# Where the zero stores stand: a mixture-of-experts layer behind chunked attention, with the gating of the last row tiles and the first loads put in another order

## The chip, the cores and the metric

The kernel runs on one core of a Trainium2 chip. The metric is the time of one execution on the device in microseconds (us); the kernel before takes 282.58 us (median of three runs, 282.15 to 282.78). A core has TensorE (PE, with its weight loads as PEld), VectorE (DVE), ScalarE (ACT), GpSimd (POOL) and SyncE (SP), which here only issues DMAs. Each engine works through its own list of instructions in order, and semaphores tie the lists together.

## The reference

`q`, `k`, `v` are 8 x 8 heads of 576 positions by 64 numbers. Attention is taken within chunks of 64 positions; its output, 4608 tokens of 512 numbers, goes through a mixture of 8 experts. A token belongs to the expert with the largest logit, an expert takes at most `capacity` (80) tokens, those with the largest gate, and all other rows of the output are zero.

```python
scores = scale * np.matmul(q_c, k_c.transpose(0, 1, 2, 4, 3))   # chunks of 64
attn = softmax(scores)
x = (attn @ v_c) as rows of 512                                 # 4608 tokens
...
logits = x @ w_gate
expert_idx = np.argmax(logits, axis=1)
gate_w = softmax(logits)[np.arange(N), expert_idx]
out = np.zeros((N, D), dtype=np.float32)
for e in range(E):
    tok_idx = the at most `capacity` tokens of expert e with the largest gate
    h = np.maximum(x[tok_idx] @ w1[e], 0.0)                     # 512 x 1024
    out[tok_idx] = gate_w[tok_idx, None] * (h @ w2[e])          # 1024 x 512
```

## The kernel before, in words

The work has three stages, one behind the other on the PE.

**Attention and gating (to about 140 us).** The tokens are 36 row tiles of 128, `i` = 0 to 35, and four of them make a group T. A load `n` brings two row tiles (`load`, L308): the queries (L318) and, for each of the two head parities, keys and values (L321), into one of four buffers `tok`. The parity's rows go to every other partition, so the other halves must be zero: `blank` (L764) clears them once at the start. The loop at L812 runs one row tile after another through a pipeline: scores of tile i (`start_scores`, L338, into `s`), attention times values of i-2 (`start_values`, L357, into `o`, copied to `x` by `keep`, L389), transposing the scores of i-1 and exp (`probs`, L382 and L384), transposing the result of i-3 (`xtrans`, L416, copied to `xT` at L417), and on DVE the maximum and the difference for tile i (`weights_of`, L368 and L371). Every fourth tile takes the logits of a group (`gate_mm`, L428; `gate_copy`, L440), normalizes it (`sums`, L396 and L398), which also stores it to the DRAM scratch `xs` from POOL (L403, L408), and transposes the logits back (`gate_sum`, L449). What follows on DVE for a group are eleven small operations: `lh` (L456), `lg` (L459) and the nine of `gate` (L506), of which the second hands an exp to ACT (L480). They are not written into the loop but wait in a list `gates`; another list, `bounds_q`, holds the search for the capacity threshold and the counting of levels (`levels` L528 to L533, `signs` L538 on ACT, `steps_` L543, `tally` L553 and L556 on PE, `left_add` L681). `fill` (L298) takes three entries from the two lists; `weights_of` calls it five times and `sums` twice, so that these small steps go between the large ones. `EARLY` (L45) says behind which tile the first six 1 MB pieces of expert weights are loaded (L759).

The loop is followed by an order written out by hand (L840 to L898): the last two tiles go through the pipeline, `gate_sum(28, 4)` puts the operations of tiles 28 to 31 aside (`late`), the token buffers are freed (L856) and SP loads w2 of expert 1 and both weights of expert 2 (`part`, L860, issued at L871). Then the small operations of tiles 28 and 32 are taken in turns, by the letters of `LAST` (L40), and all level steps follow.

**Choosing (to about 164 us).** From the threshold (`ge`, L697) over masks and ranks to the row numbers of the tokens that are kept. `keep_warm` (L727) puts matmuls without use on PE between them. All is manually ordered; an engine's instructions come in the order of the text.

**Experts (to the end).** The 8 experts have 96 slots each, six groups `r` of 128 rows, so a group takes up to three experts. `experts` (L171) gathers all six groups from `xs` by indirect DMA from POOL (L177), scales and transposes them (L188, L200), and runs layer 1 in two halves (L211, `hc`) and layer 2 (L244, `yc`), scales by the gate (L249, `ysc`) and scatters to `out` (L250). SP's loads are issued in the hook `ahead` (L1011): weights of experts 3 to 7 in the order of need, each into a buffer that the tokens or an earlier expert left, the first behind the first gather (a one-column copy by DVE, L870, carries that dependence). Between them stand the nine stores `out<-zero` (`clear`, L735, issued at L738) that put zeros into the whole output; the scatters wait for all nine.

The lists around the change, as the kernel has them:

```python
EARLY = {7: [0], 13: [1], 19: [2], 25: [3], 30: [4], 33: [5]}
...
for e, l in (((3, 0), (3, 1), (4, 0), (4, 1)), ((5, 0),), ((5, 1), (6, 0)),
             ((6, 1), (7, 0)), ((7, 1),), (), (), ())[r]:
    part(e, l, xg[0][:, 0:1] if (e, l) == (3, 0) else None)
if r < 2:
    for n in ((0, 1, 2, 3), (4, 5, 6, 7, 8))[r]:
        clear(n)
```

`(e, l)` is layer l + 1 of expert e; `ahead(0)` runs behind the gathers, `ahead(r + 1)` behind the matmuls of round r.

Of the kernel before, what the change touches and what calls it, by code (L numbers as in the profile page):

```python
# [12 lines left out]
ALU = mybir.AluOpType  # L13
# [25 lines left out]
LV, LP = 7, 8  # L39
LAST = "aaabababababababababab"  # L40
LEVEL_BY = "vavavavv"
HALVES = 32
HOT = 8

EARLY = {7: [0], 13: [1], 19: [2], 25: [3], 30: [4], 33: [5]}  # L45

# [16 lines left out]
def attention_moe(ctx: ExitStack, tc: tile.TileContext, q, kv, wg, w1, w2, cap, cst, out):  # L63
# [107 lines left out]
    def experts(pool, pp, gi, si, gate, getw, tag, extra=None):  # L171
# [64 lines left out]
        def layer2(r):  # L236
            y = (pp.tile([P, DM], F32, name=f"y{tag}{r}", tag="h", bufs=4) if extra and r == NR - 1
                 else pp.tile([P, DM], F32, name=f"y{tag}{r}", tag="y", bufs=1))
            for c in range(8):
                if c == 4 and extra and r == NR - 2:  # L240
                    hpose(NR - 1)
                for g in range(4):
                    o = 32 * g
                    nc.tensor.matmul(  # L244
                        y[o:o + 32, :], lhsT=hT[r][c // 4][:, c % 4, o:o + 32],
                        rhs=getw(groups[r][g])[1][:, c, :],
                        start=(c == 0), stop=(c == 7), tile_position=(0, o))
            ys = pool.tile([P, DM], F32, name=f"ys{tag}{r}", tag="ys", bufs=3 if extra else 1)
            nc.vector.tensor_scalar(ys, y, gate[:, r:r + 1], None, op0=ALU.mult)  # L249
            nc.gpsimd.indirect_dma_start(  # L250
                out=out, out_offset=bass.IndirectOffsetOnAxis(ap=si[:, r:r + 1], axis=0),
                in_=ys, in_offset=None, bounds_check=NT * 512 - 1, oob_is_err=False)
# [26 lines left out]
    with ExitStack() as actx:  # L279
# [28 lines left out]
        def load(n):  # L308
# [8 lines left out]
            def move(r0, r1, engs):  # L317
                engs[0].dma_start(t[:, r0:r1, 0:512], q[T, :, 2 * b + r0:2 * b + r1])  # L318
                for h in range(2):
                    c = 512 + KV * h  # L320
                    engs[1 + h].dma_start(t[h:P:2, r0:r1, c:c + KV],  # L321
                                          kv[T, h, :, 2 * b + r0:2 * b + r1])
            if n == 0:
                move(0, 1, (nc.sync, nc.sync, nc.scalar))
                move(1, 2, (nc.scalar, nc.sync, nc.sync))
            elif n == 1:
                move(0, 1, (nc.sync,) * 3)
# [34 lines left out]

        def weights_of(i):

# [398 lines left out]
        with tc.manual_schedule():  # L763
            def blank(n, r0, r1, eng):  # L764
                eng.memset(tok[n][:, r0:r1, 512:QKV], 0.0)
            blank(0, 0, 1, nc.vector)
            blank(0, 1, 2, nc.gpsimd)
            load(0)
            nc.scalar.dma_start(ident, cst[:, C_ID:C_ID + P])
            warm = gk.tile([P, 2 * P], BF16, name="warm", tag="lv", bufs=LV)  # L770
            nc.vector.memset(warm, 0.0)
            blank(1, 0, 1, nc.vector)
            blank(1, 1, 2, nc.gpsimd)
            blank(2, 0, 2, nc.vector)
            blank(3, 0, 2, nc.gpsimd)
            pw = ps2.tile([P, 256], F32, name="pw", tag="g")
# [35 lines left out]
            for i in range(RT):  # L812
# [10 lines left out]
                if i >= 3:  # L823
                    xtrans(i - 3)
                weights_of(i)
                if i >= 7 and i % 4 == 3:
# [11 lines left out]
                for n in EARLY.get(i, ()):  # L838
                    early_weights(n)
            vc = nc.vector.tensor_copy  # L840
            start_values(34)
            keep(34)
            probs(35)
            xtrans(33)
            flush(gates)
            gate_sum(28, 4)
            late = list(gates)
            gates.clear()
            sums(8, 0, 2)
            start_values(35)  # L850
            keep(35)
            flush(bounds_q)
            xtrans(34, "pt")
            xtrans(35, "m", vc)
            sums(8, 2, 4)
# [4 lines left out]
            def part(e, l, after=None):  # L860
# [10 lines left out]
                nc.sync.dma_start(w[l], (w1, w2)[l][e].rearrange("(c p) f -> p c f", p=P))  # L871
            for e, l in ((1, 1), (2, 0), (2, 1)):
                part(e, l)
            gate_mm(32, 4)
            gate_copy(32, 4)
            tails = {"a": deque(late), "b": gates}
            gate_sum(32, 4)
            for w, rt in (("a", 28), ("b", 32)):
                levels(tails[w], rt, 4)
            keep_warm(24)  # L880

            def count(rt, way):
                for j in range(rt, rt + 4):
                    if LEVEL_BY[j - 28] == way:
                        if way == "a":
                            signs(j)
                        else:
                            steps_(nc.vector, j)
            tails["a"].append((count, (28, "a")))
            tails["b"].append((count, (32, "a")))  # L890
            for w in LAST:
                step_one(tails[w])
            for w in "ab":
                flush(tails[w])
            for rt in (28, 32):
                count(rt, "v")
            for fn in S.pop('late'):
                fn()  # L898
            io_h = wk.tile([P, P, HOT], BF16, name="io_h", tag="x", bufs=3)
            nc.scalar.copy(io_h, io_b[:, P:2 * P, None].to_broadcast([P, P, HOT]))  # L900
            left_add(28, 4)
            tally(32, 4)
# [100 lines left out]
    with tc.manual_schedule():  # L1003
        with ExitStack() as ectx:
# [6 lines left out]
            def ahead(r, xg):  # L1011

                for e, l in (((3, 0), (3, 1), (4, 0), (4, 1)), ((5, 0),), ((5, 1), (6, 0)),
                             ((6, 1), (7, 0)), ((7, 1),), (), (), ())[r]:
                    part(e, l, xg[0][:, 0:1] if (e, l) == (3, 0) else None)
                if r < 2:
                    for n in ((0, 1, 2, 3), (4, 5, 6, 7, 8))[r]:
                        clear(n)

            experts(ep, pp, lambda r: gi1[:, r - 1:r] if r else gi0, si, gate, weights.get, "c",  # L1020
# [158 lines left out]
```

## Time and profile before

| | before |
|---|---|
| median of 3 runs | 282.58 us (282.15 to 282.78) |
| the profiled execution | 283.28 us |
| its span, first to last instruction | 281.5 us |
| mean granted TensorE clock | 0.951 |
| busy: PE, PEld, DVE, ACT, POOL | 249.1, 155.4, 117.6, 94.5, 57.5 us |
| DMA moved | 84.88 MB, 302 GB/s on average |
| weight loads of 2 MB | 13, 19.0 us from issue to landing (median) |

All times below are from the profiled execution, counted from its first instruction. The page gives busy time by engine, 40 equal slices of the span, the DMA queues, the chain of work that ended last, the costliest groups of instructions (`line engine operation out<-in xcount`) and the DMA issues. A row of a timeline reads: start, duration, engine, line, operation, out<-in, shape, count of merged instructions, and in brackets the engine's idle time before it and what ended it. "SPq" and "POOLq" are issues of DMAs. A DMA's "us to landing" counts from its issue until its data is there.

### The profile page before, as it was taken

How to read it: one execution, taken by the hardware profiler on the slowest of the kernel's cores; microseconds unless marked ns; L12 is line 12 of the kernel's file. 1: busy time of each engine (PE TensorE's matmuls, PEld its weight loads, DVE VectorE, ACT ScalarE, POOL GpSimd, SP SyncE). 2: the span in 40 equal slices, each digit the busy share in tenths (PEclk: the TensorE clock that was granted, in tenths of full speed). 3: DMA queues.
4: the chain of work that ended last, by engine and by line, in shares of the span. 5: the costliest groups of instructions: out<-in, count | busy, mean ns of one | idle time of the engine just before them, and what ended most of it. 6: DMA issues, size and time to landing. Idle time of an engine off the chain costs nothing. (4 is left out here: it accounts for less than half of the span.)

```text
span 281.5 us, 6470 instructions
## 1 busy us (share of the span) xinstructions
PE 249.1 (88%) x2703; PEld 155.4 (55%) x2703; DVE 117.6 (42%) x345; ACT 94.5 (34%) x194; POOL 57.5 (20%) x115
## 2 busy tenths in 40 slices
PE   4499999999999998799969969999969929999980
PEld 2488787978797877598746833333313303323320
DVE  6553465656476767437288550202010010111210
ACT  1036555556557667547825011202002001101000
POOL 9201103020202026811345360000000111010011
PEclk9999999999999999979995979999988986999997
DMA  4999899999999999640899369999999999910000
GB/s 137 350 378 398 286 352 381 381 363 406 334 386 403 349 401 367 269 154 1 239 413 408 143 200 387 398 393 404 416 403 406 404 402 400 394 72 10 3 35 34
DMA packets 31987, 84.88 MB, mean 302 GB/s; under 512 B 2576, under 2 KB 2704, under 8 KB 31952
## 3 DMA queue, kind: packets, MB, share of 16 engines
q1 hardware_dynamic: 28128, 71.32, 67.7%
q0 software_dynamic: 3456, 12.49, 11.6%
q10 hardware_dynamic: 368, 0.59, 0.9%
q8 instruction: 23, 0.38, 0.5%
q14 instruction: 12, 0.10, 0.1%
HBM read 64.07 MB, written 20.59 MB: 301 GB/s over the span
## 5 line engine op out<-in xcount | busy, mean ns | idle before, releaser
L211 PE MATMUL hc<-w,xtc 128*32 128x512 f32 x384 | 50.1, 647 | 8.2 <-SPq L1024 6.0
L338 PE MATMUL s<-tok 128*64 128x128 f32 x576 | 40.9, 287 | 4.2 <-DMA tok<-in_kv 4.2
L244 PE MATMUL yc<-w,htc 128*32 128x512 f32 x384 | 42.3, 592 | 0.0
L368 DVE TENSOR_REDUCE mx<-s 128x8 f32<-128x512 f32 x36 | 24.8, 688 | 36.8 <-PE s L338 36.3
L338 PEld LDWEIGHTS s<-tok 128*64 128x64 f32 x576 | 32.3, 141 | 13.8 <-issue 13.7
L357 PE MATMUL o<-tok,pT 128*64 128x130 f32 x576 | 38.7, 276 | 0.0
L211 PEld LDWEIGHTS hc<-w,xtc 128*32 128x32 f32 x384 | 12.7, 117 | 39.8 <-issue 29.5
L389 ACT COPY x<-o 128x520 f32<-128x520 f32 x36 | 21.3, 591 | 37.7 <-PE o L357 37.7
L357 PEld LDWEIGHTS o<-tok,pT 128*64 128x64 f32 x576 | 33.3, 137 | 1.1 <-ACT xT_last L417 0.8
L216 ACT ACTIVATE hsc<-hc 128x512 f32<-128x512 f32 x6 | 3.6, 598 | 77.9 <-PE hc L211 77.9
L244 PEld LDWEIGHTS yc<-w,htc 128*32 128x32 f32 x384 | 12.4, 110 | 28.3 <-issue 28.3
L250 POOL DMA_INDIRECT out<-ysc,si x6 | 6.0, 994 | 100.1 <-DMA out<-zero 53.3
L371 DVE TENSOR_TENSOR sm<-s,mx 128x512 f32<-128x512 f32 x36 | 24.8, 688 | 0.5
L382 PE MATMUL pt<-ct,sm 128*128 128x128 f32 x144 | 24.0, 290 | 0.0
L384 ACT ACTIVATE pT<-pt 128x512 f32<-128x512 f32 x36 | 21.5, 598 | 6.5 <-PE pt L382 5.5
L416 PE MATMUL px<-ct,x 128*128 128x128 f32 x144 | 21.9, 277 | 0.0
L417 ACT COPY xT<-px 128x512 f32<-128x512 f32 x32 | 18.6, 581 | 6.3 <-PE L L428 6.1
L382 PEld LDWEIGHTS pt<-ct,sm 128*128 128x128 f32 x144 | 15.4, 143 | 6.3 <-issue 6.1
L249 DVE TENSOR_SCALAR ysc<-yc,gatec 128x512 f32<-128x512 f32 x6 | 4.5, 751 | 33.5 <-PE yc L244 33.5
L233 DVE COPY htc<-hpc 128x512 f32<-128x512 f32 x6 | 4.2, 692 | 33.4 <-PE hpc L229 33.4
L416 PEld LDWEIGHTS px<-ct,x 128*128 128x128 f32 x144 | 17.2, 144 | 0.0
L218 DVE TENSOR_SCALAR hsc<-hc 128x512 f32<-128x512 f32 x6 | 4.1, 692 | 25.0 <-PE hc L211 25.0
(164 smaller groups left out, 255.5 us busy)
## 6 DMA issues: line engine op xcount, KB each, us to landing
w<-in_w SPq DMA_DIRECT2D x13, 2048.0 KB, 19.0
tok<-in_kv SPq DMA_DIRECT2D x32, 516.0 KB, 6.7
out<-zero SPq DMA_DIRECT2D x9, 1024.0 KB, 16.0
xs<-x POOLq DMA_DIRECT2D x8, 1040.0 KB, 10.3
tok<-in_q SPq DMA_DIRECT2D x16, 512.0 KB, 8.6
w<-in_w SPq DMA_DIRECT2D x6, 1024.0 KB, 9.4
tok<-in_kv SPq DMA_DIRECT2D x7, 258.0 KB, 5.8
xs<-x POOLq DMA_DIRECT2D x4, 260.0 KB, 9.1
```

The source lines that it names most:

```text
L211: nc.tensor.matmul(h[o:o + 32, :], lhsT=xT[r][:, b, o:o + 32], rhs=getw(groups[r][g])[0][:, b, 512 * f:512 * f + 512], start=(b == 0), sto ...
L244: nc.tensor.matmul(y[o:o + 32, :], lhsT=hT[r][c // 4][:, c % 4, o:o + 32], rhs=getw(groups[r][g])[1][:, c, :], start=(c == 0), stop=(c == ...
L250: nc.gpsimd.indirect_dma_start(out=out, out_offset=bass.IndirectOffsetOnAxis(ap=si[:, r:r + 1], axis=0), in_=ys, in_offset=None, bounds_ch ...
L338: nc.tensor.matmul(U[i]['s'][64 * u:64 * u + 64, pr], lhsT=qt[:, pr, u, :], rhs=kt[:, :, c:c + 64], start=True, stop=True)
L357: nc.tensor.matmul(po[64 * u:64 * u + 64, pr // 2, o:o + 130].rearrange("p (h e) -> p h e", h=2), lhsT=U[i]['pT'][:, pr, 64 * u:64 * u + 6 ...
L368: nc.vector.tensor_reduce(mx, d['s'], axis=AX.X, op=ALU.max)
L371: nc.vector.tensor_tensor(sm.rearrange("p c k h -> p c h k"), d['s'], mx[..., None].to_broadcast([P, 4, 2, 64]), op=ALU.subtract)
L382: nc.tensor.transpose(pt[:, pr, :], sv[:, pr, :], ident)
L384: nc.scalar.activation(pT, pt, AF.Exp, scale=0.125)
L389: copy(TT[T]['x'][:, r].rearrange("p (a c) e -> p a (c e)", a=2), U[i]['po'][:, :, 0:260])
L416: nc.tensor.transpose(pm[:, pr, :], t['x'][:, r, pr, 1:129], ident)
L417: copy(t['xT'][:, :, P * r:P * r + P], pm)
```

## The change

It has four parts.

1. The nine zero stores leave the experts' stage. A new table `CLEAR` puts them behind the token tiles 29 to 35, the first right behind the last token load, in turns with the last two early weight pieces. w1 of expert 3 is loaded with the weights of experts 1 and 2, ahead of the gather; w2 of expert 3 is now the first load behind the gather.
2. The first token load is issued by SP alone, in the order row 0, row 1; only the identity matrix is still loaded by ACT. The blanks of the first buffers are split between DVE and POOL by head parity, that of the third buffer goes to POOL whole and that of the fourth to ACT, as a copy of a zero column.
3. The loop ends ahead of `weights_of(35)`. The rest is written out anew: no small steps between the last row tile's operations; tiles 28 to 31 go through their gating and levels ahead of the last transposes (ACT copies both of these, DVE that of tile 33), their counting ahead of `gate_sum(32, 4)`; then come the operations of tiles 32 to 35 alone, with 12 instead of 24 `keep_warm` matmuls.
4. The last group's scaling by the gate is split between ACT and DVE.

```diff
-LAST = "aaabababababababababab"
...
-EARLY = {7: [0], 13: [1], 19: [2], 25: [3], 30: [4], 33: [5]}
+EARLY = {7: [0], 13: [1], 19: [2], 25: [3], 30: [4], 31: [5]}
+CLEAR = {29: [0], 30: [1], 31: [2], 32: [3, 4], 33: [5, 6], 34: [7], 35: [8]}
...
-            nc.vector.tensor_scalar(ys, y, gate[:, r:r + 1], None, op0=ALU.mult)
+            g = gate[:, r:r + 1]
+            if extra and r == NR - 1:
+                nc.scalar.activation(ys[:, 256:DM], y[:, 256:DM], AF.Copy, scale=g)
+                nc.vector.tensor_scalar(ys[:, 0:256], y[:, 0:256], g, None, op0=ALU.mult)
+            else:
+                nc.vector.tensor_scalar(ys, y, g, None, op0=ALU.mult)
...
-            if n == 0:
-                move(0, 1, (nc.sync, nc.sync, nc.scalar))
-                move(1, 2, (nc.scalar, nc.sync, nc.sync))
-            elif n == 1:
+            if n < 2:
                 move(0, 1, (nc.sync,) * 3)
                 move(1, 2, (nc.sync,) * 3)
...
-        def weights_of(i):
+        def weights_of(i, fill=fill):
...
-            def blank(n, r0, r1, eng):
-                eng.memset(tok[n][:, r0:r1, 512:QKV], 0.0)
-            blank(0, 0, 1, nc.vector)
-            blank(0, 1, 2, nc.gpsimd)
+            def blank(n, r0, r1, eng, h0=0, h1=2):
+                eng.memset(tok[n][:, r0:r1, 512 + KV * h0:512 + KV * h1], 0.0)
+            blank(0, 0, 1, nc.vector, 0, 1)
+            blank(0, 0, 1, nc.gpsimd, 1, 2)
+            blank(0, 1, 2, nc.vector, 0, 1)
+            blank(0, 1, 2, nc.gpsimd, 1, 2)
             load(0)
...
-            blank(1, 0, 1, nc.vector)
-            blank(1, 1, 2, nc.gpsimd)
-            blank(2, 0, 2, nc.vector)
-            blank(3, 0, 2, nc.gpsimd)
+            blank(1, 0, 2, nc.vector, 0, 1)
+            blank(1, 0, 2, nc.gpsimd, 1, 2)
+            blank(2, 0, 2, nc.gpsimd)
+            nc.scalar.copy(tok[3][:, :, 512:QKV],
+                           warm[:, 0:1].to_broadcast([P, 2, 2 * KV]))
...
+                if i == 35:
+                    break
                 weights_of(i)
...
+                for n in CLEAR.get(i, ()):
+                    clear(n)
             vc = nc.vector.tensor_copy
+            for n in CLEAR[35]:
+                clear(n)
+            weights_of(35, lambda: None)
+            gate_mm(28, 4)
+            gate_copy(28, 4)
+            probs(35)
             start_values(34)
             keep(34)
-            probs(35)
-            xtrans(33)
+            xtrans(33, copy=vc)
             flush(gates)
+            sums(7)
             gate_sum(28, 4)
-            late = list(gates)
-            gates.clear()
-            sums(8, 0, 2)
             start_values(35)
             keep(35)
-            flush(bounds_q)
+            sums(8, 0, 2)
+            levels(gates, 28, 4)
+            flush(gates)
             xtrans(34, "pt")
-            xtrans(35, "m", vc)
+            xtrans(35, "m")
             sums(8, 2, 4)
             qx.close()
...
-            for e, l in ((1, 1), (2, 0), (2, 1)):
+            for e, l in ((1, 1), (2, 0), (2, 1), (3, 0)):
                 part(e, l)
             gate_mm(32, 4)
             gate_copy(32, 4)
-            tails = {"a": deque(late), "b": gates}
-            gate_sum(32, 4)
-            for w, rt in (("a", 28), ("b", 32)):
-                levels(tails[w], rt, 4)
-            keep_warm(24)
...
-            tails["a"].append((count, (28, "a")))
-            tails["b"].append((count, (32, "a")))
-            for w in LAST:
-                step_one(tails[w])
-            for w in "ab":
-                flush(tails[w])
-            for rt in (28, 32):
-                count(rt, "v")
+            flush(bounds_q)
+            for way in "av":
+                count(28, way)
+            left_add(28, 4)
+            gate_sum(32, 4)
+            levels(gates, 32, 4)
+            keep_warm(12)
+            flush(gates)
+            for way in "av":
+                count(32, way)
...
-            left_add(28, 4)
             tally(32, 4)
...
-                for e, l in (((3, 0), (3, 1), (4, 0), (4, 1)), ((5, 0),), ((5, 1), (6, 0)),
+                for e, l in (((3, 1), (4, 0), (4, 1)), ((5, 0),), ((5, 1), (6, 0)),
                              ((6, 1), (7, 0)), ((7, 1),), (), (), ())[r]:
-                    part(e, l, xg[0][:, 0:1] if (e, l) == (3, 0) else None)
-                if r < 2:
-                    for n in ((0, 1, 2, 3), (4, 5, 6, 7, 8))[r]:
-                        clear(n)
+                    part(e, l, xg[0][:, 0:1] if (e, l) == (3, 1) else None)
```

## Prediction

> **What bounds the kernel now.** I read the page first, then the chain of waits, then the timeline of PE in the experts' stage, then the DMA issues of SP and the DMA traffic by window.
>
> ```profile
> span 281.5 us, 6470 instructions
> ...
> out<-zero SPq DMA_DIRECT2D x9, 1024.0 KB, 16.0
> ```
>
> The chain that ended last runs over PE matmuls of the experts (L211, L244) from 232.88 us to the last scaling, and before that hangs on a load. So the end is set by TensorE, and the question is only where TensorE is kept waiting. In its own timeline:
>
> ```profile
> 205.67 1.03 PE L211 MATMUL hc<-w,xtc 128*32 128x512 f32 x6
> 208.85 5.32 PE L211 MATMUL hc<-w,xtc 128*32 128x512 f32 x26 [2.14 <-DMA w<-in_w]
> ...
> 215.56 3.64 PE L211 MATMUL hc<-w,xtc 128*32 128x512 f32 x32
> ...
> 225.88 1.03 PE L211 MATMUL hc<-w,xtc 128*32 128x512 f32 x4
> 232.88 5.53 PE L211 MATMUL hc<-w,xtc 128*32 128x512 f32 x28 [5.97 <-SPq L1024]
> ```
>
> The undisturbed half of layer 1 (32 matmuls) takes 3.64 us. The first half for row group 3 runs from 205.67 to 208.85 + 5.32 = 214.17, that is 8.50 us: 4.86 us lost, part waiting and part at half speed after the wait. For row group 4 it runs from 225.88 to 232.88 + 5.53 = 238.41, 12.53 us: 8.89 us lost. Together 13.75 us. The first names a weight load as releaser; the second names a sequencer at the program's last `If`, which can't release a matmul here, so I take it for the weight load of expert 6 too. Why are the weights late? SP issued this:
>
> ```profile
> 108.02 1.10 SPq L759 DMA_DIRECT2D w<-in_w  x2
> 133.27 41.50 SPq L871 DMA_DIRECT2D w<-in_w  x7
> 174.87 17.31 SPq L738 DMA_DIRECT2D out<-zero  x4
> 192.29 2.66 SPq L871 DMA_DIRECT2D w<-in_w  x1
> 194.99 14.31 SPq L738 DMA_DIRECT2D out<-zero  x5
> 209.40 22.52 SPq L871 DMA_DIRECT2D w<-in_w  x5
> ```
>
> Four zero stores stand ahead of w1 of expert 5 (the load of 192.29) and five more ahead of what follows; each is 1 MB, 2.6 us at the 400 GB/s of that stage. The buffers were not what it waited for: w1 of expert 5 goes where expert 0's lay, whose last reader was done near 175 (166.37 + 4.67, a row below, and another 3.64). Between 108 and 133 SP has nothing to issue, and the traffic (40 slices of 1.525 us from 104 to 165) shows what DMA does then; below it, the us from issue to landing of weights, small stores of x and gathers of token rows:
>
> ```profile
> GB/s 401 408 376 361 338 371 419 414 255 3 0 262 385 52 11 0 0 0 5 16 208 306 314 234 373 422 420 417 419 425 411 402 396 389 340 52 0 5 185 55
> ...
> w<-in_w SPq DMA_DIRECT2D x3, 2048.0 KB, 14.6
> ...
> xs<-x POOLq DMA_DIRECT2D x4, 260.0 KB, 9.1
> ...
> xgc<-xs,gic POOLq DMA_INDIRECT x3, 3.6
> ```
>
> DMA is nearly empty from 117.7 to 134.5 and again from 157 to 165.
>
> **Part 1: zero stores and one weight load moved.** Nine stores leave the experts' stage (9.44 MB) and stand behind the last token load (about 108); w1 of expert 3 (2.10 MB) moves ahead of the gather. Nothing queues behind a new wait on SP: the zero tile is set at the start, and the two early weight loads mixed among the stores are first read after 166. The weights of experts 1 and 2 follow in the same queue.
>
> In the experts' stage nine loads remain, 5.2 us each at 400 GB/s. Even if the first starts only at 170 (below), w1 of expert 5 lands near 191, of 6 near 206 (w2 of 5, ahead of it, must wait until layer 2 of group 0 frees its buffer), of 7 near 221, against needs at about 208, 224 and 239 (205.67; 225.88 less the first wait of 4.86; their distance less that wait, 15.35, further on; each 2.6 later by the other parts). The smallest margin is some 17 us, so both waits go whole: **−13.75**, bounds −13.75 and −11 (if a shorter wait turned up elsewhere). Nothing else is late next: the rest is matmuls back to back.
>
> The cover for the moved bytes is not complete. From 104 to 165 the DMA moved about 15.0 MB (the GB/s row times 61 us); 11.5 MB more make 26.5 MB, and at 400 GB/s these end near 170, where before the weights were in by 158. The first gather is issued in the middle of that:
>
> ```profile
> 160.11 1.17 POOL L177 DMA_INDIRECT xgc<-xs,gic  x1 [3.94 <-DVE bt L951]
> ```
>
> ```profile
> 164.67 0.15 DVE L870 COPY w<-xgc 128x1 f32<-128x1 f32 x1
> ```
>
> ```profile
> 166.37 4.67 PE L211 MATMUL hc<-w,xtc 128*32 128x512 f32 x32
> ```
>
> Before, it landed 3.6 us after its issue, at 163.7; DVE, with other work until then, came to it at 164.67. Under load, from 165 on, the same page part for 165 to 260 reads:
>
> ```profile
> xgc<-xs,gic POOLq DMA_INDIRECT x4, 7.5
> out<-ysc,si POOLq DMA_INDIRECT x4, 6.3
> ```
>
> With 7.5 us (the same operation, the same load) the rows are there at 167.6 instead of 164.67: **+2.9**. Bounds: +1.7 by the scatter's 6.3, and +4.5 by the 9.1 us of the small stores of x. The stores of x themselves meet the same load, but the last is issued near 144 and has until 160.
>
> [...]
>
> **Part 2: first loads.**
>
> ```profile
> 1.23 1.78 DVE L765 MEMSET tok<- 128x2064 f32 x1 [1.23 <-PEq L1168]
> ```
>
> ```profile
> 3.03 2.11 SPq L321 DMA_DIRECT2D tok<-in_kv  x3
> ```
>
> ```profile
> 3.04 0.56 ACTq L321 DMA_DIRECT2D tok<-in_kv  x1
> 3.63 0.60 ACTq L318 DMA_DIRECT2D tok<-in_q  x1
> ```
>
> ```profile
> 10.56 1.76 PE L338 MATMUL s<-tok 128*64 128x128 f32 x14 [4.19 <-DMA tok<-in_kv]
> ```
>
> ```profile
> tok<-in_kv ACTq DMA_DIRECT2D x1, 258.0 KB, 3.4
> ```
>
> The first scores start at 10.56, released by a key/value load. Those of row 0 were issued at 3.03 and 3.04, and one of them took 3.4 us, so the start waits for the last of row 1 as well (issued until 5.14). Split between DVE and POOL the first blank takes half of 1.78, so the first key/value load goes out 0.89 us sooner, at 2.1; four more issues at about 0.62 put the last one's start at 4.6. Landing ends: 8.0 (3.4 us later, alone) and 9.67 (all as before, only 0.89 sooner). I take 8.6, nearer the first, because the constants and the second queue no longer mix with these bytes: **−2.0**, bounds −0.9 and −2.6. PE is the limit from there to the last row tile, since the token loads are eight row tiles ahead, so the gain stays. The fourth buffer's blank moves to ACT, which has nothing to compute until 16.
>
> **Part 3: the last row tiles.** Before, DVE did the gating chains of tiles 28 and 32 together, in turns:
>
> ```profile
> 141.28 0.37 ACT L440 COPY lt<-L 128x256 f32<-128x256 f32 x1 [0.45 <-PE L L428]
> 144.30 0.23 ACT L480 ACTIVATE ex<-sh 128x32 f32<-128x32 f32 x1 [2.65 <-DVE sh L479]
> ```
>
> ```profile
> 142.22 0.42 DVE L442 COPY lt<-L 128x256 f32<-128x256 f32 x1 [0.47 <-PE L L428]
> 142.56 0.41 DVE L456 TENSOR_TENSOR lh<-lT,x 128x256 f32<-128x256 f32 x1
> 143.00 0.62 DVE L459 TENSOR_REDUCE lg<-lh 128x32 f32<-128x256 f32 x1
> ```
>
> ```profile
> 142.69 0.44 PE L449 MATMUL lT<-ct,lt 128*128 128x128 f32 x2 [0.17 <-DVE lt L442]
> ```
>
> ```profile
> 146.84 0.18 DVE L488 TENSOR_TENSOR keys<-comp,gg 128x32 f32<-128x32 bf16 x1
> 147.05 0.19 DVE L528 TENSOR_TENSOR bv<-keys,lob 128x32 f32<-128x32 f32 x1
> 147.28 0.24 DVE L531 TENSOR_TENSOR bv<-bv,inw 128x32 f32<-128x32 f32 x1
> 147.55 0.18 DVE L533 TENSOR_REDUCE bo<-bv 128x4 f32<-128x32 f32 x1
> 147.65 1.06 DVE L543 TENSOR_SCALAR lv<-io_b,bo 128x256 bf16<-128x256 bf16 x5
> ...
> 149.13 0.17 DVE L697 SCALAR_TENSOR_TENSOR ge<-ph,left 128x16 bf16<-128x16 f32 x1 [0.33 <-PE ph L556]
> ```
>
> From the transposed logits of tile 32 (lT, 142.69) to the threshold (ge, 149.13) it took 6.4 us. Alone the chain is 0.41 + 0.62 + twelve steps at 0.21 (the spacing of the first two rows of the last fence), 3.55 us; then three level steps instead of five (0.6), tally and threshold (0.7): from 0.44 after lT begins, 5.3 us, a gain of 1.1. But lT comes later. In the new order, by the clock of before: DVE copies the transpose of tile 33 (0.69) until 138.0; eight short steps and a reciprocal of the queues that were left, then lh, lg and two normalizing steps of 28 bring it to 141.2; two steps more give ACT its exp, and ACT's copies of the transposes of 34 and 35 stand behind that exp, so they end at 142.8 (before: 141.4). DVE ends the chain of 28 at 143.7, normalizes (0.45) and copies lt until 144.6; two sums, two level steps and the tally of 28 stand ahead of lT on PE, which begins at 145.5 instead of 142.69. That is 2.8 later, less 1.1 gained: **+1.65**, bounds −1.1 (lT not later) and +2.6 (PE, with half the warming matmuls, at the half speed that the 232.88 row shows after a wait). The steps within are all of DVE and ACT, so no DMA load changes them.
>
> **Part 4: last scaling.**
>
> ```profile
> 273.30 0.75 DVE L249 TENSOR_SCALAR ysc<-yc,gatec 128x512 f32<-128x512 f32 x1 [6.12 <-PE yc L244]
> ```
>
> Half of it on DVE (0.42 for 256 columns, the lt row) beside half on ACT (0.37): **−0.33**, between 0 and −0.4; the scatter waits for both.
>
> **Sum.** −13.75 + 2.9 − 2.0 + 1.65 − 0.33 = −11.5. The profiled execution took 283.28 (1.78 around its span) and would take 271.8, a span of 270.0; it was 0.70 above the median of the three runs, 282.58, for which the sum gives **271.0**.
>
> **Rivals.**
> - *The gather isn't slowed.* [...] For it: stores of x under load (9.1) overtook weights issued about then (14.6). Against it: 7.5. Time 271.0 − 2.9 = 268.1.
> - *The first loads don't gain.* One queue issues the two loads that ACT issued beside it (0.56 + 0.60 = 1.16 us), more than the 0.89 gained: +0.3 instead of −2.0, 273.3. For it: SP's issues are back to back from 3.03. Against: landing, not issuing, took most of the 10.56. [...]
> - *The gather waits for all that was issued ahead of it*, until 170, landing near 171 and not 167.6: 274.4. Against: the same 9.1 beside 14.6.
> - *Slower: loads of SP starve the gathers of POOL.* The second gather (needed near 176) would come only in a gap of SP's queue, the first being where w2 of expert 5 waits for its buffer; that is after nine us of PE work and five loads, near 193: 17 us late, 288. It decides once a gather under load takes over 19 us (7.5 + 11.5). Against: 7.5 with SP's queue full.
> - *The change doesn't do what it says*: the zero stores were not what kept the weights. Then the waits stay and the other terms add up: 271.0 + 13.75 = 284.8. Against: the order of issue above.
>
> **How the numbers follow.** Chances: forecast 0.57, gather not slowed 0.14, first loads don't gain 0.14, gather behind everything 0.10, starved 0.03, waits stay 0.02. The forecast's own bounds together (gather −1.2/+1.6, head −0.6/+1.1, last tiles −2.75/+0.95) rarely all fall one way; 266.5 to 275.0 holds it and the next three cases, and leaves out the last two and the sums of extremes. 0.2% is 0.57 us, about what a measurement of this kernel tells from no change. Faster 0.94, same 0.01, slower 0.05.
>
> **What would show it.** PE in the experts' stage has no idle time over 1 us from the first layer 1 to the last; the nine stores are issued from about 106 and traffic stays near 400 GB/s until 168; the first gather takes 6 to 8 us; the first scores start between 8 and 9.7; from the first scores to ge takes longer by 1 to 2 us. Wrong would be: a wait of L211 or L244 for w, a token load that lands later than its scores, or a gather at 4 us.

## The result and the profile after

The changed kernel takes 273.01 us (median of four executions, 271.69 to 274.25) beside 282.68 (282.15 to 284.90) for the kernel before, a ratio of 0.964 (0.958 to 0.971): 9.7 us faster. The prediction said 271.0 (266.5 to 275.0). The profiled execution took 272.99; its span is 271.2, 10.3 less than before.

First the page of the changed kernel. The last column of the group rows is the idle time of PE just before such instructions.

```profile
span 271.2 us, 6450 instructions
...
L211 PE MATMUL hc<-w,xtc 128*32 128x512 f32 x384 | 45.0, 612 | 0.0
...
L244 PE MATMUL yc<-w,htc 128*32 128x512 f32 x384 | 42.3, 592 | 0.0
```

PE never waits for a weight: both layers have no idle time before them. PE's timeline shows the two places that had lost 4.86 and 8.89 us:

```profile
168.90 5.27 PE L211 MATMUL hc<-w,xtc 128*32 128x512 f32 x32
...
208.81 3.62 PE L211 MATMUL hc<-w,xtc 128*32 128x512 f32 x32
...
224.14 3.62 PE L211 MATMUL hc<-w,xtc 128*32 128x512 f32 x32
```

The first half of layer 1 now takes 3.62 us in groups 3 and 4, the undisturbed time. SP's queue (start, time until the last of the run is issued):

```profile
108.20 0.60 SPq L740 DMA_DIRECT2D out<-zero  x1
...
112.45 22.50 SPq L740 DMA_DIRECT2D out<-zero  x7
135.05 89.65 SPq L885 DMA_DIRECT2D w<-in_w  x13
```

The zero stores are issued by 135 and thirteen weight loads follow with no store between them. The DMA traffic from 104 to 165, in the same 40 slices as for the kernel before, has no gap left; below it, from the same window, the count, size and median us from issue to landing:

```profile
GB/s 394 401 380 327 246 357 403 420 416 391 419 422 400 413 419 400 389 404 408 407 406 418 388 407 403 312 363 398 376 353 343 396 371 410 422 415 399 389 384 396
...
w<-in_w SPq DMA_DIRECT2D x4, 2048.0 KB, 25.4
...
xs<-x POOLq DMA_DIRECT2D x4, 260.0 KB, 12.4
...
xgc<-xs,gic POOLq DMA_INDIRECT x4, 7.5
```

The gather is issued into that traffic, and DVE, which copies a column of its rows, waits for it:

```profile
159.33 1.17 POOL L177 DMA_INDIRECT xgc<-xs,gic  x1 [3.93 <-DVE bt L961]
```

```profile
167.21 0.15 DVE L884 COPY w<-xgc 128x1 f32<-128x1 f32 x1 [3.38 <-DMA xgc<-xs,gic]
```

The marks at the head, at the last row tile and at the end, from PE's, DVE's, ACT's and POOL's timelines:

```profile
10.51 0.91 PE L340 MATMUL s<-tok 128*64 128x128 f32 x6 [4.13 <-DMA tok<-in_kv]
...
129.77 1.09 PE L340 MATMUL s<-tok 128*64 128x128 f32 x16
...
254.66 7.91 PE L244 MATMUL yc<-w,htc 128*32 128x512 f32 x72
```

```profile
148.32 0.17 DVE L699 SCALAR_TENSOR_TENSOR ge<-ph,left 128x16 bf16<-128x16 f32 x1 [0.40 <-PE ph L558]
...
263.15 0.48 DVE L252 TENSOR_SCALAR ysc<-yc,gatec 128x256 f32<-128x256 f32 x1 [6.62 <-ACT ysc L251]
```

```profile
262.64 0.47 ACT L251 ACTIVATE ysc<-yc,gatec 128x256 f32<-128x256 f32 x1 [10.32 <-PE yc L244]
```

```profile
263.91 0.98 POOL L255 DMA_INDIRECT out<-ysc,si  x1 [6.12 <-DVE ysc L252]
```

Of the kernel before, two marks are still missing, from PE's and POOL's timelines (its last layer-2 matmul ended at 273.24, 0.06 ahead of its scaling):

```profile
131.25 1.09 PE L338 MATMUL s<-tok 128*64 128x128 f32 x16
```

```profile
274.33 0.98 POOL L250 DMA_INDIRECT out<-ysc,si  x1 [5.88 <-DVE ysc L249]
```

Cut at these marks, the two spans compare like this:

| stretch, us | before | after | difference | predicted |
|---|---|---|---|---|
| start to first scores | 10.56 | 10.51 | -0.05 | -2.0 |
| to the scores of tile 35 | 120.69 | 119.26 | -1.43 | 0 |
| to `ge` | 17.88 | 18.55 | +0.67 | +1.65 |
| to the first gather's issue | 10.98 | 11.01 | +0.03 | 0 |
| to DVE's first use of its rows | 4.56 | 7.88 | +3.32 | +2.9 |
| to the first layer 1 | 1.70 | 1.69 | -0.01 | 0 |
| to the end of the last layer 2 | 106.87 | 93.67 | -13.20 | -13.75 |
| to the last scatter's issue | 1.09 | 1.34 | +0.25 | -0.33 |
| to the end of the span | 7.17 | 7.29 | +0.12 | 0 |

The large terms are as predicted. The first loads, the last scaling and an unforeseen -1.43 in the token stage are not.

### The profile page after: what moved, and what is told of

It reads as the page before. It is cut to its first block, busy times and chain, and to the rows that moved or that the text cites. A ratio compares the mean times of both kernels' runs of the same rounds, so it can differ in the third digit from the quotient of the medians.

```text
span 271.2 us, 6450 instructions
## 1 busy us (share of the span) xinstructions
PE 241.2 (89%) x2691; PEld 151.6 (56%) x2691; DVE 115.0 (42%) x345; ACT 98.3 (36%) x196; POOL 57.8 (21%) x116
## 4 chain that ended last, share of the span: by engine, by line
PE 80%; DMA 10%; ACT 3%; DVE 2%; POOL 2%; issue 1%; POOLq 0%; ACTq 0%
PE hc L211 16%; PE yc L244 15%; PE s L340 13%; PE o L359 11%; PE pt L384 7%; PE px L418 5%; DMA xs<-x 4%; PE L L430 3%; DMA xgc<-xs,gic 3%; PE hpc L229 2%; DMA tok<-in_kv 2%; ACT lv L540 2%; POOL tok L767 1%; PE xpc L200 1%; PE lT L451 1%; PE pwarm L734 1%
## 5 line engine op out<-in xcount | busy, mean ns | idle before, releaser
L211 PE MATMUL hc<-w,xtc 128*32 128x512 f32 x384 | 45.0, 612 | 0.0
L211 PEld LDWEIGHTS hc<-w,xtc 128*32 128x32 f32 x384 | 12.0, 112 | 27.4 <-issue 27.0
L254 DVE TENSOR_SCALAR ysc<-yc,gatec 128x512 f32<-128x512 f32 x5 | 3.8, 752 | 27.3 <-PE yc L244 27.3
L499 POOL TENSOR_TENSOR comp<-comp,ct 128x32 bf16<-128x32 bf16 x18 | 3.9, 233 | 48.1 <-DVE comp L513 41.2
## 6 DMA issues: line engine op xcount, KB each, us to landing
w<-in_w SPq DMA_DIRECT2D x6, 1024.0 KB, 10.3
```

Source lines behind the costliest of these rows:

```text
L211: nc.tensor.matmul(h[o:o + 32, :], lhsT=xT[r][:, b, o:o + 32], rhs=getw(groups[r][g])[0][:, b, 512 * f:512 * f + 512], start=(b == 0), sto ...
```

## The experiments

Each kernel is the changed one with the edit shown, if nothing else is said; times are medians of six executions (twelve of the last head experiment), with the ratio to the kernel before run beside them.

### Part 1 alone, on the kernel before

```diff
-EARLY = {7: [0], 13: [1], 19: [2], 25: [3], 30: [4], 33: [5]}
+EARLY = {7: [0], 13: [1], 19: [2], 25: [3], 30: [4], 31: [5]}
+CLEAR = {29: [0], 30: [1], 31: [2], 32: [3, 4], 33: [5, 6], 34: [7], 35: [8]}
...
+                for n in CLEAR.get(i, ()):
+                    clear(n)
...
-            for e, l in ((1, 1), (2, 0), (2, 1)):
+            for e, l in ((1, 1), (2, 0), (2, 1), (3, 0)):
...
-                for e, l in (((3, 0), (3, 1), (4, 0), (4, 1)), ((5, 0),), ((5, 1), (6, 0)),
+                for e, l in (((3, 1), (4, 0), (4, 1)), ((5, 0),), ((5, 1), (6, 0)),
...
-                if r < 2:
-                    for n in ((0, 1, 2, 3), (4, 5, 6, 7, 8))[r]:
-                        clear(n)
```

> The kernel before with part 1 of the change alone (zero stores behind tiles 29 to 35, (3,0) ahead of the gather, (3,1) first behind it). Theory: all of the gain is part 1's. By the two traces the experts' stage gives 13.2 and the gather takes back 3.3, so 9.9 faster than the kernel before: 273.1 (272.5 to 273.8), with no wait of PE for weights from the first layer 1 to the end. Rival (the other parts carry some of it): 274.5 or more.

273.26 us, 0.965 (0.962 to 0.969), against the whole change's 0.964 (0.958 to 0.971). All that PE waits for between 165 and 262, in the view of waits (total, times, longest), is the gather's rows:

```profile
PE xpc L201 <- DVE xnc L189: 5.2, 1, 5.2
```

So part 1 carries the gain, and the other three parts together move the time by nothing that can be told.

### The loads that stand in the gather's way

```diff
-            for e, l in ((1, 1), (2, 0), (2, 1), (3, 0)):
+            for e, l in ((1, 1),):
...
-                for e, l in (((3, 1), (4, 0), (4, 1)), ((5, 0),), ((5, 1), (6, 0)),
+                for e, l in (((2, 0), (2, 1), (3, 0), (3, 1), (4, 0), (4, 1)), ((5, 0),), ((5, 1), (6, 0)),
```

> The change, but with the loads of (2,0), (2,1) and (3,0) taken from ahead of the gather to behind it, (2,0) now the one that waits for it; (1,1) stays early. Theory (the first gather shares the DMA engines with the weights): the last early load, (1,1), lands at about 158, so the engines are empty when the gather is issued at about 159.3; it lands after 3.6 to 4.5 us instead of 7.9, layer 1 starts about 3.4 us earlier, the weights come 4 to 5 us later than in the changed kernel, which its 5 to 16 us of slack takes in, and the time falls from 273.0 to 269.6 (269 to 270.3). Rival A (the gather is late for another reason, such as its rows' stores to xs): it still takes 7 to 8 us and the time is 273.0 or above. Rival B (the loads are only just in time): the gather is quick, but waits of layer 1 and layer 2 for weights come back, over 1 us each, and the time is 271.5 to 274.

273.29 us, 0.967 (0.964 to 0.969): no gain. The gather, issued at 159.30, was used at 163.96 (DVE's timeline), 3.2 us less than in the changed kernel, which settles that it paid for the traffic beside it:

```profile
163.96 0.15 DVE L884 COPY w<-xgc 128x1 f32<-128x1 f32 x1 [0.17 <-issue]
```

Where the gain went stands in PE's timeline:

```profile
165.40 5.34 PE L211 MATMUL hc<-w,xtc 128*32 128x512 f32 x32
...
205.98 1.03 PE L211 MATMUL hc<-w,xtc 128*32 128x512 f32 x6
208.75 3.62 PE L211 MATMUL hc<-w,xtc 128*32 128x512 f32 x26 [1.73 <-DMA w<-in_w]
```

Layer 1 started 3.5 us earlier (165.40 instead of 168.90). At group 3 PE waited for w1 of expert 5, and group 4 began where it had in the changed kernel (224.08, 224.14). With the engines kept empty for the gather's sake (122 GB/s from 162 to 166), the later loads moved back: DMA, at 384 to 399 GB/s from 172 to 230, is the bound behind PE. Rival B of the expectation was right on this. The next kernel holds back two loads instead of three:

```diff
-            for e, l in ((1, 1), (2, 0), (2, 1), (3, 0)):
+            for e, l in ((1, 1), (2, 0)):
...
-                for e, l in (((3, 1), (4, 0), (4, 1)), ((5, 0),), ((5, 1), (6, 0)),
+                for e, l in (((2, 1), (3, 0), (3, 1), (4, 0), (4, 1)), ((5, 0),), ((5, 1), (6, 0)),
```

> The change, but with (2,1) and (3,0) alone taken behind the gather; (2,0) stays early. Theory (DMA is the bound until about 230, so an idle stretch of it moves all later weights by its length, and the gather is slow only while weights are in flight): (2,0) lands at about 164, the gather between 4 and 5.5 us after its issue, the engines idle some 3 us instead of the 8 in the experiment that holds three, (5,0) lands at about 204, ahead of its need at about 206: 1.5 to 2.5 us faster than the change, 270.5 to 271.5. Rival A (a single 2 MB load in flight slows the gather as much): 6.5 to 8 us for the gather, 272.5 to 273. Rival B (the weights again come too late): a wait of over 1 us in layer 1 of group 3, 272 to 273.

270.65 us, 0.958 (0.955 to 0.961): 2.4 us faster than the change. The gather, issued at 160.44, was used 4.58 us later, and group 3 ran without a wait:

```profile
166.46 3.64 PE L211 MATMUL hc<-w,xtc 128*32 128x512 f32 x32
...
204.74 3.80 PE L211 MATMUL hc<-w,xtc 128*32 128x512 f32 x32
```

One 2 MB load less to make up for (5.2 us at 400 GB/s) decides between no gain and most of it. Whether a single load in flight would slow the gather was not tried: here the last one was nearly done when the gather was issued.

### The last row tiles in the order of before

```diff
-                if i == 35:
-                    break
...
+            probs(35)
...
+            late = list(gates)
...
+            for w in LAST:
+                step_one(tails[w])
```

> The change, but with the last row tiles in the order of before (part 3 undone; the ninth zero store stays behind tile 35). Theory from the two traces (scores of tile 35 to ge 17.88 us before, 18.55 us after): 0.7 us faster, 272.3. The prediction's size: 1.65 faster, 271.4. Rival (part 3 is a gain, or nothing, and the difference lay in single executions): 273.0 or slower, with 18.3 us or more from the scores of tile 35 to ge.

273.54 us, 0.965 (0.963 to 0.968): by the time alone, the same as the change. The stretch itself says more. From PE's and DVE's timelines, 131.49 to 149.38:

```profile
131.49 1.09 PE L341 MATMUL s<-tok 128*64 128x128 f32 x16
```

```profile
149.38 0.17 DVE L700 SCALAR_TENSOR_TENSOR ge<-ph,left 128x16 bf16<-128x16 f32 x1 [0.33 <-PE ph L559]
```

This is 17.89 us. The three profiled kernels with the order of before have 17.87 to 17.89, the six with the changed order, leaving out those that move the sums (below), 18.38 to 18.63. So part 3 costs 0.5 to 0.75 us. The time of this execution (273.56) doesn't show it, because it lost 1.3 us ahead of this stretch, where the granted clock was 0.60 from 120 to 124 (below).

### The last scaling on DVE alone

```diff
-            if extra and r == NR - 1:
-                nc.scalar.activation(ys[:, 256:DM], y[:, 256:DM], AF.Copy, scale=g)
-                nc.vector.tensor_scalar(ys[:, 0:256], y[:, 0:256], g, None, op0=ALU.mult)
-            else:
-                nc.vector.tensor_scalar(ys, y, g, None, op0=ALU.mult)
+            nc.vector.tensor_scalar(ys, y, g, None, op0=ALU.mult)
```

> The change, but with the last group's scaling by the gate on DVE alone (part 4 undone). Theory (the halves run one behind the other, DVE waits for ACT): the end of the last matmul to the last scatter's issue takes 1.1 us instead of 1.34, and the time is 0.25 faster, 272.75. Rival (the prediction's term): 0.33 slower, 273.3.

272.37 us, 0.963 (0.960 to 0.965): 0.6 us below the change, less than the spread of either kernel's times (2.6). PE ended at 261.37; then, in DVE's timeline and POOL's:

```profile
261.44 0.75 DVE L250 TENSOR_SCALAR ysc<-yc,gatec 128x512 f32<-128x512 f32 x1 [6.12 <-PE yc L244]
```

```profile
262.47 0.98 POOL L251 DMA_INDIRECT out<-ysc,si  x1 [5.88 <-DVE ysc L250]
```

1.10 us from the end of PE to the scatter, against 1.34 with the split. The rows of the change show why: ACT's half ran from 262.64 to 263.11, and DVE's began at 263.15, named as released by ACT. Two halves one behind the other (0.47 + 0.48) are longer than the whole (0.75). That is an order of the program: DVE's half waits for the semaphore that ACT's half raises, so the chip was never asked to do both at once. Both halves read one PSUM tile, and no run here shows what they would do there without the wait. Whether halves in two tiles would overlap was not tried.

### The first loads

```diff
-            if n < 2:
+            if n == 0:
+                move(0, 1, (nc.sync, nc.sync, nc.scalar))
+                move(1, 2, (nc.scalar, nc.sync, nc.sync))
+            elif n == 1:
...
-            blank(0, 0, 1, nc.vector, 0, 1)
-            blank(0, 0, 1, nc.gpsimd, 1, 2)
+            blank(0, 0, 1, nc.vector)
+            blank(0, 1, 2, nc.gpsimd)
```

> The change, but with the first loads and the blanks of before (part 2 undone). Theory from the two traces: the first scores start at 10.56 instead of 10.51, no difference in time, 273.0 (272.8 to 273.3). Rival (the prediction's term, and the execution of the changed kernel that was profiled was an unlucky one): 2.0 slower, 275.0.

275.09 us, 0.969 (0.965 to 0.973). The first scores start at 10.56 as in the kernel before, 0.05 from the change:

```profile
10.56 0.70 PE L343 MATMUL s<-tok 128*64 128x128 f32 x4 [4.19 <-DMA tok<-in_kv]
```

The median lies 2.1 above the change's, but not by the step that the prediction named. The start scatters: nine profiled kernels with the changed head start their scores between 9.86 and 10.92, the three with the head of before between 10.34 and 10.56. In the profiled execution 1.20 of it lie between the first scores and those of tile 35, where PE's clock fell by half for a stretch (0.57 on average from 120 to 124; below), and 0.54 in the first half of layer 1 (5.81 instead of 5.27). Of six executions two took 272.6 and 272.9, four 274.9 to 276.2. Whether half the clock is likelier here, or six executions fell so by chance, is open.

What holds the first load up? In the next kernel almost nothing runs beside it: the blanks of the other buffers, and so all later loads but one piece of 256 KB (queries, issued at 5.01), wait until it has landed.

```diff
-            blank(1, 0, 2, nc.vector, 0, 1)
-            blank(1, 0, 2, nc.gpsimd, 1, 2)
-            blank(2, 0, 2, nc.gpsimd)
-            nc.scalar.copy(tok[3][:, :, 512:QKV], ...)
+            for n, eng in ((1, nc.vector), (2, nc.gpsimd)):
+                eng.tensor_copy(tok[n][:, :, 512:QKV:KV], tok[0][:, :, 512:QKV:KV])
+            blank(1, 0, 2, nc.vector)
+            blank(2, 0, 2, nc.gpsimd)
+            blank(3, 0, 2, nc.gpsimd)
```

> The change, but the blanks of the token buffers 1 to 3 wait until the first load has landed (DVE and POOL copy four of its columns first), and with them all later loads; DVE blanks the second buffer, POOL the third and fourth. Theory A (writes of POOL, DVE and ACT to SBUF slow the first load's DMAs down): its last piece lands 3.6 to 4 us after its issue at 4.4 instead of 6, the first scores start at 8.2 to 8.7. Theory B (the second load's DMAs, in flight beside it, do it): the same. Theory C (a start-up time of the DMA itself): the first scores stay at 10.5 (9.9 to 10.9). In A and B the time is 271 if the second load lands before the third row tile needs it at about 17.5; if not, PE waits there.

282.0 us, 0.997 (0.994 to 1.000). The chain of waits of the change has the first of these rows, that of this kernel the second (start, time until landing):

```profile
4.38 5.99 DMA tok<-in_kv
```

```profile
4.37 4.71 DMA tok<-in_kv
```

So with almost nothing beside it the last piece still needs 4.71 us, and the scores start at 9.22. That is neither 8.2 to 8.7 nor 10.5: what runs beside the first load costs 1.3 us in this pair, 0.6 to 1.7 by the scatter of the changed head. Which of the blanks and the second load does it is open, and so is whether another order of issue would start below 9.2. The DMA windows show where the time goes: from 5.5 to 7.5 us, with pieces issued at 3.2 to 4.4 still on their way, DMA moved 123 GB/s in the change and 237 here, and 390 from 9.0 to 10.5 in the change. Why it is slow there is not shown. The second load, whose keys and values are issued 8.1 us later (13.82 instead of 5.73), then made PE wait:

```profile
9.22 3.47 PE L340 MATMUL s<-tok 128*64 128x128 f32 x32 [2.83 <-DMA tok<-in_kv]
21.60 1.98 PE L340 MATMUL s<-tok 128*64 128x128 f32 x16 [5.68 <-DMA tok<-in_kv]
```

The scores of tile 35 came at 139.00 instead of 129.77: the whole 9 us went to the end. Time that PE lost at the head of the stage was not made up.

### Sums of the counts later

From the first scores to those of tile 35 it took 120.0 to 120.7 us in the kernel before, in part 1 alone, with the last tiles or the first loads undone and with two loads held, but 119.3 to 119.4 in the change, with three loads held and with the scaling undone, though PE runs the same instructions there. The windows of 120 to 124 (busy time and count by engine, then PE's clock, DMA share, GB/s), first of the kernel before, then of the change:

```profile
120.00:124.00 4.00, 4.00 (x36) 3.66 (x33) 1.86 (x5) 1.34 (x3) 0.72 (x1) 0.59 0.68 263
```

```profile
120.00:124.00 4.00, 4.00 (x60) 3.66 (x58) 1.86 (x5) 2.42 (x6) 0.81 (x1) 1.00 1.04 415
```

At half clock PE did 36 matmuls where it otherwise did 60. From 112 to 130 the mean clock was 0.91 in the four others that took 120.0 us or more and 1.00 in the three that took less. Just ahead, PE waits in both kernels (view of waits of the change, 106 to 124):

```profile
PE ph L558 <- ACT lv L540: 2.7, 5, 1.1
PE ph L558 <- DVE left L683: 0.3, 1, 0.3
```

The tally of a group's counts stands on PE right behind the last of ACT's signs for it. This kernel puts the next group's signs between, with two more buffers:

```diff
-LEVELS = {15: "l0:4 c0 c1 c2 - - - - s2 c3", 19: "l4:5 - s3 s0 c4", 23: "l5:6 s4 s1 c5",
-          27: "l6:7 s5 c6 - - - - - s6"}
-LV, LP = 7, 8
+LEVELS = {15: "l0:4 c0 c1 c2 - - - - c3 s2", 19: "l4:5 s0 c4 s3", 23: "l5:6 s1 c5 s4",
+          27: "l6:7 c6 s5 - - - - - s6"}
+LV, LP = 9, 8
```

> The change, but with the counts of levels of tiles 8 to 27 summed on PE later, the next count's signs in between, and two more buffers for the signs (9 instead of 7). Theory (PE's five waits of 2.7 us together for ACT's signs, between 111.9 and 118.7, are on the path, and their idle time is what brings the half-clock stretch of 3.4 us behind them in some executions): from the first scores to those of tile 35 in 116.3 instead of 119.3, no half clock between 115 and 130, 2.5 to 3 us faster, 270.0 to 270.5, and less scatter. Rival A (ACT or DVE is the bound there, and the wait only moves): 119 again, 273. Rival B (the later sums are missed at the end, in the flush of the list): up to 1 us more from the scores of tile 35 to ge.

268.04 us, 0.949 (0.946 to 0.952): 5 us faster than the change, and more than expected. PE's scores of tile 35 start 114.45 us behind the first instead of 119.26. The windows from the first scores to those of tile 35, of the change and of this kernel:

```profile
10.51:129.77 119.26, 116.06 (x1518) 97.25 (x1518) 71.18 (x211) 69.29 (x143) 25.45 (x63) 1.00 1.01 373
```

```profile
10.21:124.66 114.45, 114.38 (x1518) 96.46 (x1518) 72.08 (x213) 69.17 (x143) 25.88 (x65) 0.99 1.01 376
```

PE runs the same 1518 matmuls. Of 119.26 us it was not busy for 3.20, of 114.45 for 0.07: 3.1 of the 4.8 us are waits that are gone. The other 1.7 are busy time, 116.06 against 114.38. Half of that are the matmuls of the tallies themselves (busy us, mean ns, then idle before), in the change and here:

```profile
L558 PE MATMUL ph<-comp,lv 128*128 128x8 bf16 x40 | 2.8, 168 | 3.2 <-ACT lv L540 2.7 <-DVE left L683 0.5
```

```profile
L558 PE MATMUL ph<-comp,lv 128*128 128x8 bf16 x40 | 1.9, 166 | 0.0
```

Each takes as long as before, 166 ns beside 168, but those that came one by one behind a wait now overlap: forty of them make 1.9 us of busy time. The other 0.8 lies at the head, ahead of any tally: from the first scores to the next row tile's it took 4.73 us instead of 5.54, most of it in eight matmuls without use. So about 4.0 us belong to the sums, and 0.8 to the head of these two executions. The stretch to `ge` stayed at 18.57. So the waits were on the path of the changed kernel; the kernel before has the same 2.7 and 0.3 us of them.

### Together

```diff
+CLEAR = {29: [0], 30: [1], 31: [2], 32: [3], 33: [4], 35: []}
...
+                for e, l in (((3, 0), (3, 1), (4, 0), (4, 1)), ((5, 0),), ((5, 1), (6, 0)),
...
+                for n in ((5, 6), (7, 8))[r] if r < 2 else ():
+                    clear(n)
```

With the later sums and the scaling on DVE alone:

> Three findings together: the sums of the counts later (as in the experiment tallies_later); five zero stores among the token tiles and four behind the gather, two behind (4,1) and two behind (5,0), with (3,0) the load that waits for the gather; the last scaling on DVE alone. Theory: the early loads are done by about 152, the gather (issued at about 153.5) lands in 3.6 to 4.6 us instead of 8.0, the last scaling gives 0.25 back, and since no DMA time is lost, all later weights still land ahead of their need: 268.0 - 3.8 - 0.25 = 264 (263.2 to 264.8). Rival (the late zero stores bring the waits of the kernel before back): waits of PE for weights of over 1 us in groups 2 to 4, 265.5 to 268.

264.88 us, 0.938 (0.934 to 0.941), the best of the study and 8.1 below the change. The gather, issued at 154.81, was used at 159.37, and in the view of waits PE waits once from 160 to the end, for the gather's rows:

```profile
PE xpc L200 <- DVE xnc L188: 2.1, 1, 2.1
```

Four zero stores do stand among the experts' weights here, and no weight is late. Two variants of it:

> The same with the last row tiles in the order of before. Theory (that order is 0.6 us shorter from the scores of tile 35 to ge): 0.6 faster than all_three, 263.4. Rival (with the sums later, more of the list is left for the end, where before's order has no room for it): equal or slower than all_three.

266.44 us, 0.942 (0.938 to 0.947), and 18.82 us from the scores of tile 35 to `ge` instead of 18.56: with the sums later, no advantage of the order of before is left to see, as the rival said. How much it lost can't be told from one execution: the next kernel runs the same instructions as the best one up to `ge`, and took 18.96.

> all_three with 18 more matmuls without use on PE ahead of the wait for the gather. Theory (the half clock in the first layer 1 comes from PE's idle time while it waits for the gather): the first half of layer 1 of group 0 takes 3.7 to 4.3 us instead of 4.7 to 5.4, 0.5 to 1 us faster than all_three, 263.2. Rival (the matmuls hold up the sum behind them and, through DVE, the scaling of the gathered rows): equal or slower.

265.63 us, 0.938 (0.934 to 0.941), no difference. The rival's mechanism is in the trace: DVE came to the gathered rows 6.37 us behind the gather's issue instead of 4.56, since the sum that its next steps read stood behind the added matmuls. The theory's sign is there too, the first half of layer 1 in 3.64 us instead of 5.34, the time of such a half at a granted clock of 1.00 (kernel before, 215.56 to 219.20), but the added matmuls are not shown to be its cause: with two loads held, the same half took 3.64 without them.

## Why the prediction was right, and where it was not

**The stalls.** "Both waits go whole: -13.75" was right: they are gone. The 0.55 that are missing go with the first half of layer 1, 5.27 instead of 4.67 us, longer at half clock (0.50 until 172.3, 3.4 us of this half, and until 168.5 in the kernel before, 2.1 us). The length of the wait for the gather doesn't explain that: over the profiled kernels this half took 3.64 to 6.13 us, 5.34 behind a short wait (three loads held) and 4.78 behind a long one (last tiles undone). The margin was smaller than the predicted 17 us: w1 of expert 5, issued at 178.37, took 20.6 us and landed 9.8 ahead of group 3, where 191 was expected. With three loads held back it landed at 208.7, and group 3 waited.

**The gather.** +2.9 predicted, +3.32 measured: read off the row of 7.5 us for gathers beside weight loads, it landed 7.86 us after its issue. Two experiments took the traffic away and got 3.2 and 3.3 us back, so the rival in which the gather isn't slowed is refuted. So is the wait behind everything issued: all four weight loads issued in that window ahead of the gather took 23.2 to 31.3 us, and the last two landed at 172.2 and 178.0, behind the gather's 167.2.

**The first loads.** This step failed. The issue was as predicted (last one at 4.38, predicted 4.6). The landing was not: "I take 8.6, nearer the first" put about 4 us on a piece that needed 5.99, and 4.71 with almost nothing beside it. The 3.4 us came from one of the two earliest key and value pieces, when few others were in flight. The rival that the first loads don't gain described the outcome, though not by the issue times that it named.

**The last row tiles.** The sign was right, the size was 0.67 and not 1.65. The step "lT comes later" was mis-sized. In the change lT begins at 142.63 (PE's timeline), 12.86 behind the scores of tile 35; before it was 142.69, 11.44 behind:

```profile
142.63 0.63 PE L451 MATMUL lT<-ct,lt 128*128 128x128 f32 x4
```

That is 1.4 later, not 2.8, and from there to `ge` 5.69 instead of 6.44, a gain of 0.75, not 1.1.

**The last scaling.** -0.33 predicted, +0.25 measured. The step "half of it on DVE beside half on ACT" failed: DVE's half waits for ACT's, and the halves run one behind the other.

**The token stage.** -1.43 was not in the sum. It is mainly the stretch at half clock, which the profiled execution of the change did not have; part 1 alone has it and is as fast. No part of the change is shown to remove it, and taking away the waits ahead of it took it away as well: five of eight profiled kernels with these waits have it (not counting the one whose first load runs alone), none of the four without.

Against the sum, the first loads came out 1.95 worse, the last scaling 0.58, the stalls 0.55, the gather 0.42; the last tiles 0.98 better, the token stage 1.43; the rest is 0.14 worse. Together 1.2: a span of 271.2 where the sum gave 270.0. The median, 273.01, is 2.0 above the forecast and inside its range. Most of the error is the one step of the first loads. That the sum comes out so near is partly luck: -1.43 of the token stage, which no part of the change is shown to give, and 0.98 of the last tiles, together more than the first loads missed, stand on the other side. The median lies next to the 273.3 of the rival that gives the first loads no gain.

## What to carry to other kernels

A store that nobody reads soon still has a place in a queue: look for the stretch in which DMA is empty, and count what it then delays there, above all a small gather on the path. When a transfer on the path runs beside bulk loads, take its duration from rows under load (here 7.5 us, and 3.6 without), and hold back just so many loads as have slack; one too many gives the gain back (270.65 us with two held, 273.29 with three). Times of parts that move less than a microsecond are read from marks in the trace, since the whole time scatters more than that (2.6 us here); and since a mark scatters too (18.56 and 18.96 us for the same instructions here), from several executions.

## What the runs showed of the hardware

- A gather of 128 rows landed 3.6 us after its issue with the DMA engines nearly idle (kernel before, 81 GB/s until it had landed) and 7.5 in the median with them full (the change, 390 GB/s until the first had landed), while weight loads of that window took 25.4. In seven kernels with full engines DVE came to the rows 6.8 to 8.2 us after the issue, in the four that hold loads back for it, without added matmuls, 4.6 to 4.7.
- The granted clock falls to half, for 3.4 us or twice as long in the two traces of before and after. In the kernel before it is 0.50 from 121.0 to 124.0, with 0.71 and 0.88 in the half microseconds on either side, so 3.4 us in all; further stretches of 3.4 us end at 168.5 and 212.9, one of 6.8 at 236.8. In the change one of 6.8 ends at 172.3. Ahead of the first one of the kernel before, PE had waited 0.96, 0.22, 0.22 and 0.27 us, 1.7 together, between 116.7 and 119.5, and worked between the waits. What makes the clock fall is not shown. From 112 to 130 its mean was 0.91 in some executions and 1.00 in others, with the same instructions; how much the stretch makes of the 2.6 us by which the times of the change scatter is open.
- A scaling split between ACT and DVE behind a semaphore took 0.47 and 0.48 us, with 0.04 us between the end of one half and the start of the other; the whole on DVE took 0.75.
